# Folding q's weights in 32x32 tiles in the first token tile, and a new order around it

## The chip, the cores and the metric

The kernel runs on one core of a Trainium2 chip. The metric is the time of one execution on the device in microseconds (us). The kernel before took 374.88 us, the median of three runs (374.73 to 374.95). The engines are named as the profile does: PE (matrix products), PEld (PE's loads of the stationary operand), DVE, ACT and POOL (elementwise work), SP (which here only issues DMA transfers, in the order of its queue).

## What is computed

```python
# x: 2048 tokens x 512; 32 heads of 16 features
q, k, v = split_heads(x @ wqkv)
pq = einsum("bhsd,hdf->bhsf", q, w_phi)
pk = einsum("bhsd,hdf->bhsf", k, w_phi)
phi_q = concat([softmax(pq), softmax(-pq)])
phi_k = concat([softmax(pk), softmax(-pk)])
kv = einsum("bhsf,bhsd->bhfd", phi_k, v)
z = einsum("bhsf->bhf", phi_k)
num = einsum("bhqf,bhfd->bhqd", phi_q, kv)
den = einsum("bhqf,bhf->bhq", phi_q, z)[..., None] + 1e-6
a = merge_heads(num / den) @ wo
# second branch: per head the best of 16 keys on each side picks one of 256 experts
s1 = einsum("nhc,ec->nhe", x @ w_q[..., :128], k1)
s2 = einsum("nhc,ec->nhe", x @ w_q[..., 128:], k2)
e = argmax(s1) * 16 + argmax(s2)
b = sum over heads of gelu(x . u[e]) * v[e]
g = sigmoid((x * gate_w).sum(-1))
out = g * a + (1 - g) * b
```

## The kernel before

The 2048 tokens are cut into 16 tiles of 128. Every fp32 product is made of three products of a high and a low part (`mm3`), so each operand exists twice: `xh` and `xl`, `wah` and `wal`, `sh` and `sl`, `uh` and `ul`. One projection of a tile by 512 columns is 12 matmuls (4 blocks of 128 rows, 3 products each).

**Folded weights.** The key and query projections are not followed by `w_phi`; the product of the two weights is made once, on the chip, in `fold` (line 149), for k in the prologue and for q in tile 15. `fold` takes 64 matmuls of 32 rows, with the raw weights (`raw`) stationary and the small `wd` (32 columns made from `w_phi`, line 283) moving, into four banks (one for each group `q` of 8 heads), in two halves that are yielded one by one. ACT then casts them to `wah`, and DVE subtracts for `wal`. k's folded weights live in `wah` and `wal`; in tile 15 q's take their place.

**Score weights.** For the second branch the weights of `w_q` are multiplied with the keys in the same way (`score_w`, line 218): 16 loads of 1 MB (`wq0` to `wq15`, two buffers of the tag `st`, which the raw weights of k and q use as well), each multiplied in four matmuls with 512 columns, two loads to a bank `ws0` to `ws7`. A full bank goes through ACT as 16-bit planes (`score_planes`, line 226: `wpl`), is turned by a DMA transposition on SP (`wtp`), put together by ACT (`score_join`, line 233: `wtj`, then `sh`) and split by POOL (`sl`).

**The loop** (line 311) runs over the 16 tiles. Tile t loads x of tile t+3 (`x_load`), projects v (`vproj`, `pv`) and k (`kproj`, `pk`), takes the differences to the maximum and the minimum on DVE (`softmax_diffs`), the exponent on ACT, the sum, reciprocal and scaling (`ksoft`, line 196: DVE, DVE, POOL), and in every second tile adds two tiles to the sums of k and v (`kvacc`). The table `plan` (line 309) says how many loads of score weights each tile multiplies; after each, the load after next is issued on SP, where it waits until the product that reads its buffer is over. Everything is emitted under a schedule written by hand: each engine works its rows in the order of the program, and SP its transfers.

**The transition.** In tile 15 come the two halves of q's fold, between them the two halves of tile 0's scores (`front_s`: `s0`, `s1`), `kvacc(13)` and the sums of k for the last two tiles (`kvz`, line 211). Then the second loop runs tile by tile (`a` = 0 to 13, line 755) through q's projection (`front_q`), the projections to u and the gate (`front_p`, `pp`), the softmax of q, gelu, the choice of the experts, and the output product `po`. `z_split`, `z_rows` and `z_spread` (from line 695) bring the sum `z` into the rows that the denominators need.

## Time and profile before

| what | value |
|---|---|
| time, median of three runs | 374.88 us |
| time of the profiled execution | 375.19 us |
| its span, first to last instruction | 373.4 us |
| granted clock of PE | 1.000 |
| HBM read, written | 26.39 MB, 4.19 MB |
| mean traffic of the DMA engines | 125 GB/s |

The profile is of one execution. Its span begins with the first instruction and ends with the last; 1.8 us of the execution's time lie outside it. Busy times of engines overlap, so their sum says nothing; what counts is which engine's work and waits make up the chain that ended last. In the rows below and in the prediction, "x64" is a count of instructions in the trace; an fp32 matmul appears there twice, so that `fold`'s half of 32 matmuls is listed as 64. Names are the program's with the number left out (`foldq` is any of the four banks). "idle before, releaser" says how long the engine stood before these instructions, and which instruction of another engine released it.

### The profile page before, as it was taken

How to read it: one execution, taken by the hardware profiler on the slowest of the kernel's cores; microseconds unless marked ns; L12 is line 12 of the kernel's file. 1: busy time of each engine (PE TensorE's matmuls, PEld its weight loads, DVE VectorE, ACT ScalarE, POOL GpSimd, SP SyncE). 2: the span in 40 equal slices, each digit the busy share in tenths (PEclk: the TensorE clock that was granted, in tenths of full speed). 3: DMA queues.
4: the chain of work that ended last, by engine and by line, in shares of the span. 5: the costliest groups of instructions: out<-in, count | busy, mean ns of one | idle time of the engine just before them, and what ended most of it. 6: DMA issues, size and time to landing. Idle time of an engine off the chain costs nothing.

```text
span 373.4 us, 9179 instructions
## 1 busy us (share of the span) xinstructions
PE 367.6 (98%) x3680; PEld 294.3 (79%) x3680; DVE 314.4 (84%) x750; ACT 236.5 (63%) x421; POOL 161.5 (43%) x170
## 2 busy tenths in 40 slices
PE   8999999999999999999999999999999999999995
PEld 4767587787777888888888888888888888888874
DVE  4458878767767888999999999999999999999983
ACT  4243567437438544585876876966966966968752
POOL 2104363344343734573363453543643642743740
PEclk9999999999999999999999999999999999999999
DMA  7469894595695033143515434424326254245101
GB/s 269 172 235 300 226 305 173 147 303 180 169 289 194 4 87 80 35 101 77 103 20 84 110 60 84 101 58 98 89 69 100 70 87 98 62 96 100 58 29 58
DMA packets 71819, 46.52 MB, mean 125 GB/s; under 512 B 63200, under 2 KB 64096, under 8 KB 69472
## 3 DMA queue, kind: packets, MB, share of 16 engines
q1 hardware_dynamic: 70912, 45.17, 46.8%
q10 hardware_dynamic: 864, 0.76, 0.8%
q8 instruction: 29, 0.48, 0.5%
q14 instruction: 14, 0.11, 0.1%
HBM read 26.39 MB, written 4.19 MB: 82 GB/s over the span
## 4 chain that ended last, share of the span: by engine, by line
PE 93%; DMA 4%; ACT 1%; DVE 1%; issue 0%; ACTq 0%; DVEq 0%
PE po L629 17%; PE s L61 7%; PE s L60 7%; PE s L59 6%; PE pq L60 4%; PE pq L61 4%; PE pv L61 4%; PE ws L223 4%; PE pv L60 3%; PE pk L61 3%; PE pk L60 3%; PE pq L59 3%; PE pv L59 3%; PE oT L518 3%; PE s L57 3%; PE kvacc L207 2%
## 5 line engine op out<-in xcount | busy, mean ns | idle before, releaser
L439 POOL TENSOR_TENSOR w<-d,zb 128x512 f32<-128x512 f32 x32 | 40.8, 1296 | 80.6 <-ACT d L433 78.2
L200 POOL TENSOR_TENSOR d<-d,st 128x1024 f32<-128x1024 f32 x16 | 31.1, 1943 | 65.9 <-DVE st L199 58.5
L61 PE MATMUL s<-sh,xl 128*128 128x480 f32 x128 | 48.6, 380 | 0.0
L60 PE MATMUL s<-sl,xh 128*128 128x480 f32 x128 | 48.5, 379 | 0.0
L433 ACT ACTIVATE d<-d 128x512 f32<-128x512 f32 x32 | 20.0, 631 | 42.5 <-DVE d L109 34.1
L467 POOL TENSOR_TENSOR d<-d,st 128x512 f32<-128x512 f32 x30 | 31.3, 1064 | 23.0 <-DVE st L460 19.6
L509 ACT COPY pt<-tp 128x1024 uint16<-128x1024 uint16 x28 | 36.6, 1375 | 0.9 <-DMA tp<-pl 0.8
L59 PE MATMUL s<-sh,xh 128*128 128x480 f32 x96 | 36.4, 379 | 0.0
L353 ACT ACTIVATE d<-d 128x1024 f32<-128x1024 f32 x16 | 17.0, 1063 | 27.5 <-DVE d L111 27.5
L499 ACT COPY pl<-d 128x1024 uint16<-128x1024 uint16 x28 | 29.2, 1045 | 3.1 <-POOL d L467 3.1
L61 PEld LDWEIGHTS s<-sh,xl 128*128 128x128 f32 x128 | 24.0, 188 | 4.1
L60 PEld LDWEIGHTS s<-sl,xh 128*128 128x128 f32 x128 | 24.1, 188 | 3.3
L198 DVE TENSOR_REDUCE st<-d 128x64 f32<-128x1024 f32 x16 | 19.5, 1219 | 6.6 <-ACT d L353 6.3
L61 PE MATMUL pk<-wah,xl 128*128 128x480 f32 x64 | 24.3, 380 | 0.0
L60 PE MATMUL pk<-wal,xh 128*128 128x480 f32 x64 | 24.3, 379 | 0.0
L60 PE MATMUL pq<-wal,xh 128*128 128x480 f32 x64 | 24.3, 379 | 0.0
L61 PE MATMUL pq<-wah,xl 128*128 128x480 f32 x64 | 24.2, 379 | 0.0
L61 PE MATMUL pv<-wbh,xl 128*128 128x512 f32 x60 | 23.8, 397 | 0.3 <-DVE xl L145 0.3
L629 PE MATMUL po<-wbh,xh 128*128 128x512 f32 x60 | 23.7, 395 | 0.0
L629 PE MATMUL po<-wbl,xh 128*128 128x512 f32 x60 | 23.5, 392 | 0.0
L60 PE MATMUL pv<-wbl,xh 128*128 128x512 f32 x60 | 23.5, 392 | 0.0
L476 DVE TENSOR_TENSOR eq<-s,mx 128x512 bf16<-128x512 f32 x32 | 22.1, 692 | 1.1
(218 smaller groups left out, 1057.8 us busy)
## 6 DMA issues: line engine op xcount, KB each, us to landing
wq<-wq SPq DMA_DIRECT2D x16, 1024.0 KB, 6.8
xr<-xT SPq DMA_DIRECT2D x15, 256.0 KB, 6.2
y<-ot SPq DMA_DIRECT2D x15, 256.0 KB, 2.1
rawk<-wkT SPq DMA_DIRECT2D x1, 1024.0 KB, 6.4
rawq<-wqT SPq DMA_DIRECT2D x1, 1024.0 KB, 5.7
rawo<-wo SPq DMA_DIRECT2D x4, 256.0 KB, 3.9
rawu<-ug SPq DMA_DIRECT2D x2, 258.0 KB, 5.9
rawv<-wv ACTq DMA_DIRECT2D x2, 256.0 KB, 4.7
```

Of the source, the lines that this page charges most:

```text
L59: pe.matmul(o_, ah, bh[:, r], start=False, stop=False)
L60: pe.matmul(o_, ah, bl[:, r], start=False, stop=False)
L61: pe.matmul(o_, al, bh[:, r], start=False, stop=(last and i == n - 1))
L198: dve.tensor_reduce(st[:, 64:128], g64(d), axis=AX.X, op=ALU.add)
L200: pool.tensor_tensor(g64(d), g64(d), b64(st[:, 128:192]), op=ALU.mult)
L433: act.activation(hs(d, i), hs(d, i), AF.Exp)
L439: pool.tensor_tensor(hs(e["w"], i), hs(e["ph"], i), hs(zb, i), op=ALU.mult)
L467: eng.tensor_tensor(g64(d)[:, gs_], g64(d)[:, gs_], r[:, gs_].unsqueeze(2).to_broadcast([P, 32, F]), op=ALU.mult)
L476: dve.tensor_tensor(e["eq"][:, 512 * half:512 * half + 512].rearrange("p (h f) -> p h f", f=F), p3, mx.unsqueeze(2).to_broadcast([P, H, F] ...
L499: act.copy(pl, e["ph"][:, halves[i]].bitcast(U16).rearrange("p (c j) -> p j c", j=2))
L509: act.copy(p16[:, :, 4 * i:4 * i + 4, :], e["tp"][i].rearrange("p (j g) n -> p j g n", j=2))
L629: pe.matmul(h["po"], lhs(), rhs, start=first, stop=last)
```

## The change

q's fold moves from tile 15 to tile 0 and is computed another way. `fold_rows` makes the `wd` tile stationary and the raw weights moving: 16 matmuls of 32 rows by 32 columns of the array and 512 moving columns, one for each row group and output group, into four banks `foldq0` to `foldq3`. The result has features in rows, so it is turned like the score weights are: ACT writes planes, SP transposes them by DMA, ACT joins and casts to `wqh`, POOL subtracts for `wql`. Groups 0 and 1 are turned in tile 0, 2 in tile 2, 3 in tile 3; joined in tiles 2 to 5. q's folded weights have buffers of their own now; `uh`, `ul`, `eh` and `el` lie over k's weights (`shared`) and are split in tile 15, by ACT and POOL.

The raw weights of q take the first load's place, and the score weights follow one load later by a new table. `wpl` and `wtp` have two buffers each. x of tile 3 is split ahead of the loop by DVE; v of tile 3 moves to tile 2, of tiles 12 and 13 to tiles 13 and 14. `ksoft(14)` moves behind the differences of tile 15. In the transition `kvz(15)` stands between `pq0` and `pp0`, and `z_split`, `z_rows`, `z_spread`, `gelu_act(0)` and `back_cl(0)` change places.

```diff
+    shared = per.tile([P, 2 * NK * NU + 4 * D], F32R, name="shared")
+    wah, wal = part(0, NK, D), part(NK * D, NK, D)
+    uh, ul = part(0, NK, NU), part(NK * NU, NK, NU)
+    eh, el = part(2 * NK * NU, 2, D), part(2 * NK * NU + 2 * D, 2, D)
...
+    def fold_rows(raw):
+        for q in range(4):
+            qf[q] = tr_bank(f"foldq{q}") if q else mm_bank("foldq0")
+        for b in range(NK):
+            for q in range(4):
+                r = slice(32 * q, 32 * q + 32)
+                pe.matmul(qf[q][32 * b:32 * b + 32, :], wd[r, b, :], raw[r, b, :], start=True, stop=True,
+                          skip_group_check=True)
...
+    def turn_planes(src, n_):
+        pl = wa_.tile([P, 2, D], U16, tag="wpl", bufs=2, name=f"wpl{n_}")
+        act.copy(pl, src.bitcast(U16).rearrange("p (c j) -> p j c", j=2))
+        tp = wa_.tile([P, 8, P], U16, tag="wtp", bufs=2, name=f"wtp{n_}")
         sp.dma_start_transpose(tp, pl.rearrange("p j c -> p (j c)"))
+        return tp
+
+    def turn_join(tp, n_, hi, lo):
+        tj = wa_.tile([P, D], F32, tag="wtj", bufs=1, name=f"wtj{n_}")
         act.copy(tj.bitcast(U16).rearrange("p (k n j) -> p j k n", j=2, n=P),
                  tp.rearrange("p (j k) n -> p j k n", j=2))
+        t3 = tj.rearrange("p (k h e) -> p k h e", k=NK, e=F)
+        act.copy(hi, t3)
+        pool.tensor_tensor(lo, t3, hi, op=ALU.subtract)
...
-    raws = [stage(wq[0], "wq0")]
-    raws.append(stage(wq[1], "wq1"))
+    x_split(3)
+    raws = [stage(wqT, "rawq")]
+    raws.append(stage(wq[0], "wq0"))
...
-    plan = {0: 2, 2: 1, 3: 1, 4: 2, 6: 2, 8: 2, 10: 2, 12: 2, 13: 1, 14: 1}
+    plan = {2: 1, 4: 2, 5: 1, 6: 2, 7: 2, 8: 1, 9: 2, 10: 1, 11: 2, 12: 2}
...
+        if t == 2:
+            vproj(3)()
+        if t in (NT - 3, NT - 2):
+            vproj(t - 1)()
...
         for _ in range(plan.get(t, 0)):
-            score_w(done, raws[done])
+            score_w(done, raws.pop(0))
             done += 1
-            if done + 1 < 16:
-                raws.append(stage(wq[done + 1], f"wq{done + 1}"))
-            elif done == 15:
-                rawq = stage(wqT, "rawq")
+            used()
             if done % 2 == 0:
                 score_planes(done // 2 - 1)
+        if t == 0:
+            fold_rows(raws.pop(0))
+            used()
+            tq = []
...
-            for k in range(2):
-                split(eh[:, k, :], el[:, k, :], rawe[k], pool)
-            fq = fold(rawq, wah, wal, "q", False)
-            next(fq)
+        if t == NT - 1:
+            for k in range(NK):
+                split(uh[:, k, :], ul[:, k, :], rawu[k // 2][:, k % 2, :], pool)
+            split(eh[:, 0, :], el[:, 0, :], rawe[0], pool)
+            rawe.append(spare(ev[:, 1], "rawe1", [P, D]))
             front_s(0, 0)
-            next(fq)
             front_s(0, 1)
             kvacc(NT - 3)
-            next(fq)
+        if t == NT - 1:
+            ksoft(t - 1)
         act.activation(phis[t], phis[t], AF.Exp)
-        if t == 13:
-            for k in range(NK):
-                split(uh[:, k, :], ul[:, k, :], rawu[k // 2][:, k % 2, :])
-            rawe.append(spare(ev[:, 1], "rawe1", [P, D]))
-        ksoft(t)
+        if 1 < t < 6:
+            q_join(t - 2, tq[t - 2])
+        if t != NT - 2:
+            ksoft(t)
+        if t < 4:
+            tq += [q_planes(q) for q in ((0, 1), (), (2,), (3,))[t]]
```

Three places show how the order moves; two of them are on PE, one on SP. In a row, the number behind a name counts the program's tiles.

On PE before, around tile 12 (`ws6`, `ws7` the last two banks of score weights, of `wq12` to `wq15`; `pv13`, `pk13`, `pk14` projections, of which the first matmul of 12 is given):

```order
L223 MATMUL ws6_1219<-wq12_1051,kp_78 32x512 x4
L223 MATMUL ws6_1219<-wq13_1057,kp_78 32x512 x4
L207 MATMUL kvacc_98<-v9_977,d9_993 32x17 x32
L207 MATMUL kvacc_98<-v10_1024,d10_1040 32x17 x32
L57 MATMUL pv13_1308<-wbh_71,xh_61 128x512
L57 MATMUL pk13_1324<-wah_69,xh_61 128x512
L223 MATMUL ws7_1343<-wq14_1224,kp_78 32x512 x4
L57 MATMUL pk14_1368<-wah_69,xh_61 128x512
L223 MATMUL ws7_1343<-wq15_1230,kp_78 32x512 x4
```

And in the changed kernel, from the end of tile 11 to tile 13:

```order
L231 MATMUL ws6_1221<-wq12_1055,kp_75 32x512 x4
L231 MATMUL ws6_1221<-wq13_1104,kp_75 32x512 x4
L57 MATMUL pk12_1252<-shared_67,xh_61 128x512
L231 MATMUL ws7_1271<-wq14_1226,kp_75 32x512 x4
L231 MATMUL ws7_1271<-wq15_1232,kp_75 32x512 x4
L215 MATMUL kvacc_95<-v9_1018,d9_1034 32x17 x32
L215 MATMUL kvacc_95<-v10_1078,d10_1094 32x17 x32
L57 MATMUL pk13_1360<-shared_67,xh_61 128x512
L57 MATMUL pv12_1379<-wbh_68,xh_61 128x512
```

The products of `wq14` and `wq15` have moved up: one projection stands between them and the products of `wq12` and `wq13`, where two projections and two sums, and then another projection, stood before.

On SP, the transfers from the end of the prologue to tile 5 in the changed kernel (`xr` x tiles, `wtpq0` to `wtpq3` the transposed planes of q's fold, `wtp0` those of `ws0`):

```order
L135 DMA wq2_421<-wq 128x2048
L238 DMA_TRANSPOSE wtpq2_467<-wplq2_465 128x8x128
L141 DMA xr6_469<-xT 128x512
L238 DMA_TRANSPOSE wtpq3_502<-wplq3_500 128x8x128
L141 DMA xr7_504<-xT 128x512
L135 DMA wq3_545<-wq 128x2048
L238 DMA_TRANSPOSE wtp0_549<-wpl0_547 128x8x128
L135 DMA wq4_556<-wq 128x2048
L141 DMA xr8_632<-xT 128x512
L135 DMA wq5_673<-wq 128x2048
```

Before, the loads `wq2` to `wq4` had one transposition among them, that of `ws0`; now `wq3` stands behind that of `wtpq3`, which is issued once ACT has written the planes of group 3.

On PE at the transition, the changed kernel from tile 15's last sums to the first projection of u (first matmul of each projection; in the program before, 32 matmuls of `foldq` stood ahead of `s0_0` and 32 ahead of `s1_0`, and `kvz(15)` behind `pp0`):

```order
L57 MATMUL pk15_1507<-shared_67,xh_61 128x512
L57 MATMUL s0_0_1538<-sh_63,xh_61 128x512
L57 MATMUL s1_0_1551<-sh_63,xh_61 128x512
L215 MATMUL kvacc_95<-v13_1439,d13_1373 32x17 x32
L223 MATMUL kvacc_95<-ones_71,d14_1420 32x1 x32
L57 MATMUL pq0_1655<-wqh_65,xh_61 128x512
L223 MATMUL kvacc_95<-ones_71,d15_1520 32x1 x32
L57 MATMUL pp0_1700<-shared_67,xh_61 128x258
```

The sums of tile 14 by `ones` (fifth row) read `d14`, whose scaling now comes behind the differences of tile 15 on DVE.

## The prediction

> **What bounds the kernel now.** I read the page first, its busy times and the chain that ended last.

> ```profile
> PE 367.6 (98%) x3680; PEld 294.3 (79%) x3680; DVE 314.4 (84%) x750; ACT 236.5 (63%) x421; POOL 161.5 (43%) x170
> PE 93%; DMA 4%; ACT 1%; DVE 1%; issue 0%; ACTq 0%; DVEq 0%
> ```

> PE is busy for 98% of the span and carries 93% of the chain. Next come the waits of PE, which here is the whole answer, and the busy time of PE by stretches (columns: length, then busy and count for PE, PEld, DVE, ACT, POOL, clock, DMA share, GB/s).

> ```profile
> PE warm L269 <- POOL tab L253: 1.2, 1, 1.2
> PE pv L92 <- ACT wbh L49: 0.5, 1, 0.5
> PE pv L61 <- DVE xl L145: 0.3, 1, 0.3
> 20.40:43.00 22.60, 22.29 (x174) 15.51 (x173) 16.66 (x25) 9.92 (x12) 7.04 (x4) 1.00 0.91 289
> 43.00:336.70 293.70, 293.70 (x3038) 239.59 (x3042) 261.89 (x634) 196.57 (x341) 136.72 (x132) 1.00 0.47 114
> 336.70:373.40 36.70, 32.91 (x300) 26.69 (x299) 26.95 (x76) 22.44 (x52) 14.17 (x15) 1.00 0.23 62
> ```

> From 43 to 336.7 us PE never stands. In the loop's first four tiles it waits once, 0.3 us. So three rules follow. Matmul time taken out is worth its full length. Work taken off DVE and ACT in that stretch is worth nothing, since nothing there waits for them. And every new wait of PE is paid in full, since there is no slack behind it to swallow it.

> **What goes: the old fold at tile 15.** The chain has its two halves whole, and two windows hold them and a half of s of tile 0 alone.

> ```profile
> 118.03 1.92 PE foldq L163 x64
> 119.95 0.43 PE s L57
> 122.77 1.92 PE foldq L163 x64
> 124.69 0.43 PE s L57
> 118.03:127.51 9.48, 9.48 (x160) 8.10 (x162) 6.98 (x12) 7.33 (x10) 6.82 (x6) 1.00 0.12 24
> 144.16:146.78 2.62, 2.62 (x14) 2.25 (x12) 2.45 (x8) 2.59 (x5) 1.68 (x2) 1.00 0.44 100
> ```

> 9.48 - 2 x 2.62 = 4.24 us: two halves of the fold of 1.92 each, and 0.2 us each for the matmul behind, 0.43 long and not 0.22, because the array changes its tiling. Ten score-weight sites plus two halves make 12 such changes before; one new fold, ten sites and the sums of v and k of tiles 11 and 12, which now stand alone, make 12 after. So the 0.2s cancel and **-3.84** is left. The fold's four ACT casts and four DVE subtractions beside it were covered: PE waits for neither.

> **What comes: 16 matmuls of 32x32 tiles at tile 0.** No row has this form. The nearest: a score-weight product, four matmuls (8 in the trace) of the same 512 columns and type, running in four column tiles side by side; and oT, where eight tiles run at once.

> ```profile
> 100.67 1.85 PE ws L223 x16
> 102.52 1.14 PE kvacc L207 x79
> 103.66 0.43 PE pv L57
> 106.62 0.23 PE pk L57
> 109.24 1.00 PE ws L223 x8
> 163.73 0.67 PE L518 MATMUL oT<-pt,kvb 64*32 64x128 f32 x32
> ```

> A round of four costs 1.85 / 2 = 0.93. If all 16 tiles run at once, the 16 matmuls cost that plus some issue; if only four at a time, 4 x 0.93 = 3.7. oT speaks for more than four at a time: its 32 instructions of 128 columns are as many columns as a ws round's 8 of 512, but take 0.67 where the round takes 0.93. At oT's eight tiles and pace the new fold would cost 4 x 0.67 = 2.7, and at sixteen half of that, 1.34; by the ws row, whose instructions are as long as the new ones, 0.93. I take **+1.07**, near the ws row; bounds 0.93 and 3.7. Its evictions (planes, joins) lie on ACT, POOL and SP, beside full PE work; they cost nothing but where SP's queue hands them on, at tile 5 below. xl of tile 4 is made earlier, so the 0.3 us wait goes: **-0.3**.

> **Score weights closer together: tile 12.** Two 1 MB buffers serve these loads; a load starts when the product that reads its buffer is over. The DMA queue's rows and the loads issued in two windows around the pair that starts at S = 100.67:

> ```profile
> 101.73 1.19 SPq L134 DMA_DIRECT2D wq<-wq  x2
> wq<-wq SPq DMA_DIRECT2D x1, 1024.0 KB, 4.7
> wq<-wq SPq DMA_DIRECT2D x1, 1024.0 KB, 8.0
> DMA to landing us min/median/max: 4.7/6.8/8.6
> ```

> The first load is issued at S+1.06 and lands at S+5.76; the second is issued at S+1.92 (an issue takes 0.33) and, sharing the engines, lands at S+9.92. Before, their readers came at 109.24 (S+8.57) and at 113.07, with v, k and sums between. The changed order has only pk12 between the two pairs. PE has the pair done at S+1.85 and pk12 (106.62 to 109.24: 2.62, plus 0.2) at S+4.67. It waits 1.1 for wq14, works to S+6.7, and waits 3.2 for wq15: **+4.3**. Bounds: at the shortest landing in the trace, 4.7, for both, 1.1; at the longest, 8.6, for the second, 4.9. I take the rows of the pair, since this is the same event. Behind the waiting product stand the sums of tiles 9 and 10 and pk13; all of PE shifts.

> [...] The trace's pair took until S+9.92, 8.9 us after the first issue, and I stay with it.

> **A load behind a transposition: tile 5.** The load of wq3 may start when the first product of tile 4's pair has ended, but on SP it stands behind the transposition of q3's planes, the last of the new fold, and that waits for ACT. The starts of pk0 and of the product behind it, the pace of DVE, and what ACT and SP do for one such turn:

> ```profile
> 20.57 0.23 PE pk L57
> 23.20 1.90 PE ws L223 x16
> 28.86 0.63 DVE L105 TENSOR_REDUCE st<-pk 128x32 f32<-128x512 f32 x1
> 34.11 0.63 DVE L105 TENSOR_REDUCE st<-pk 128x32 f32<-128x512 f32 x1
> 35.84 0.68 DVE L111 TENSOR_TENSOR d<-st,pk 128x512 f32<-128x512 f32 x1
> L353 ACT ACTIVATE d<-d 128x1024 f32<-128x1024 f32 x16 | 17.0, 1063 | 27.5 <-DVE d L111 27.5
> L235 ACT COPY wtj<-wtp 128x1024 uint16<-128x1024 uint16 x8 | 10.8, 1351 | 2.7 <-DMA wtp<-wpl 2.5 <-POOL sl L241 0.2
> L240 ACT CAST sh<-wtj 128x512 fp32r<-128x512 f32 x8 | 9.0, 1125 | 0.3
> L228 ACT COPY wpl<-ws 128x1024 uint16<-128x1024 uint16 x8 | 8.1, 1012 | 8.9 <-PE ws L223 8.8
> 40.15 1.25 SPq L230 DMA_TRANSPOSE wtp<-wpl  x1
> ```

> DVE cycles a tile in 5.25 (28.86 to 34.11), so tile 3's differences start near 39.36 and end 2.41 later (34.11 to 36.52) at 41.8. ACT then does the exponent 1.06, the join of q1 1.35 + 1.13 and the planes of q3 1.01: 46.3. The transposition holds SP 1.25, the x tile's issue behind it some 0.4: wq3 goes out at 48.0. PE reaches its product at 23.20 + fold 1.27 + four pk (2.62) + pv3, pv4, pv5 (2.76: 106.62 less 103.66, less 0.2) + three score-weight products 2.85 + sums of tiles 0 to 2, 1.7 + two refills 0.4 + pk5 2.62 = 50.8. With landing times of 4.7 to 6.8, the wait is 1.9 to 4.0; nothing less unless ACT runs earlier. I take **+2.6**, a landing of 5.4, nearer the short end, since only the transposition and one x tile of 256 KB are in flight when it starts.

> Tiles 6 and 7 hold two pairs with the sums of tiles 3 and 4, pv7 and pk7 between: PE is at the last product at S + 1.85 + 1.34 + 2.76 + 2.62 + 1.0 = S+9.6, its load at S+9.92: **+0.4**, bounds 0 and 0.9.

> **Transition.** ksoft of tile 14 moves behind the differences of tile 15.

> ```profile
> L198 DVE TENSOR_REDUCE st<-d 128x64 f32<-128x1024 f32 x16 | 19.5, 1219 | 6.6 <-ACT d L353 6.3
> L199 DVE RECIPROCAL st<-st 128x64 f32<-128x64 f32 x16 | 8.9, 553 | 0.5
> L200 POOL TENSOR_TENSOR d<-d,st 128x1024 f32<-128x1024 f32 x16 | 31.1, 1943 | 65.9 <-DVE st L199 58.5 <-ACT wtj L235 7.4
> L401 POOL TENSOR_TENSOR x<-x,px 128x256 f32<-128x256 f32 x16 | 11.9, 746 | 3.7 <-ACT x L392 3.6
> L50 POOL TENSOR_TENSOR el<-rawe,eh 128x512 fp32r<-128x512 f32 x2 | 2.6, 1334 | 0.0
> ```

> With pk15 ended at T, d of tile 14 is scaled at T + 2.41 + 1.22 + 0.55 + 1.94 = T+6.1, T+6.3 with handovers. PE, two halves of s (5.24) and the sums of tile 13 (half of 1.14) later, needs it at T+5.8: **+0.5**. Behind it on PE stand pq0, the sums of tile 15 and pp0, in order. POOL has five pieces ahead of that scaling, u's split moved from DVE and half of the value table's: 4 x 0.75 + 1.33 = 4.3 by the rows of like size. u lies over k's weights now, so its casts wait until pk15 has read them, and the first pieces come free while pk15 runs; POOL is done near T+3.8, before the reciprocal at T+4.2. If none started before T, it would be T+4.7 and the wait 1.0; if handovers cost nothing, 0.3. The z steps, the gelu and the back part of tile 0 move on ACT, DVE and POOL only or to places where PE has 2.6 us of other matmuls ahead of them: nothing; if that cover failed anywhere, PE would stand there and the waits of PE would list it.

> **Sum.** -3.84 + 1.07 - 0.3 + 4.3 + 2.6 + 0.4 + 0.5 = +4.73 on a span of 373.4, so 378.1. The profiled execution took 375.19, 1.8 outside the span and 0.3 over the median of 374.88. I set the change on the median: **379.6 us**.

> **Rivals.** *wq3 in time.* ACT reaches q3's planes 3 us sooner, if exponents and joins overlap more than their mean times say. Against it stands the queue of DVE, which the 5.25 us cycle fixes. Without the terms of tiles 5 and 7: 379.6 - 3.0 = 376.6. Chance 0.16.

> *Faster: loads that keep their 4.7.* If the second load of a pair does not slow down, wq15 lands at S+1.92+4.7 = S+6.6, before PE needs it; the turning point is a landing of 4.8 us. Then tile 12 costs 1.1, tiles 5 and 7 at best nothing: -3.84 + 1.07 - 0.3 + 1.1 + 0.5 = -1.5, so 373.4. For it: the first of the pair took 4.7. Against it: the second took 8.0. Chance 0.10. With tile 5's wait at 1.9 beside it, 375.3, within the resolution: 0.05.

> *Four tiles at a time.* The fold costs 3.7: 382.2. The oT row speaks against it. Chance 0.08.

> *The clock falls in a gap*, or the transition waits longer. The clock reads 1.00 in each window, in the last one too, where PE idles 36.70 - 32.91 = 3.8 us in pieces. If a gap of 3.2 us at tile 12 halved it for as long again, about 3.4 us of matmuls would take 1.7 more: 381.3. Chance 0.06. [...]

> That the change doesn't do what it says holds in part within my forecast: it frees DVE and ACT at the transition, where no one waits for them.

> **How the numbers follow.** My forecast has 0.55. About 0.2%, 0.75 us, is what a measurement of this kernel can tell from no change. Faster: the second rival and a little of the first's spread, 0.11; within: its variant, 0.06; slower: the rest, 0.83. The range leaves out the fast rival below and the far ends above, 375.6 to 382.3; the likeliest case alone spans 378.2 to 381.2.

> **What will show it.** Right: waits of PE's weight loads for wq near 1.1 and 3.2 us at tile 12, 2 to 4 at tile 5; foldq as 32 instructions in about 1 us; kvz behind POOL by half a microsecond; clock 1.00. Wrong, if wq lands with PE not waiting at tile 12, if foldq takes over 2 us, or if PE idles past tile 15 for an engine that was free before.

## The result and the profile after

The changed kernel took 386.79 us, the median of four executions (385.03 to 392.81), against 374.86 before: a ratio of 1.030, 95% interval 1.024 to 1.037. The ratio leaves out the slowest execution, 392.81, as a slow one (the median of the other three is 385.16); the first profile fell in it, so the rows here are of the second one, 390.34 us with a span of 388.5. Run again beside other kernels it took 387.69 (385.35 to 390.34) against 374.96: 1.034 (1.028 to 1.040). The forecast was 379.6, with a range up to 382.3: the sign was right, the size outside.

The page, its busy times, the clock in 40 slices and the chain:

```profile
span 388.5 us, 8997 instructions
PE 371.7 (96%) x3584; PEld 294.8 (76%) x3584; DVE 310.6 (80%) x743; ACT 247.6 (64%) x428; POOL 170.4 (44%) x178
PEclk9999989999696999999999999999999999999999
PE 88%; DMA 7%; DVE 2%; ACT 1%; issue 1%; POOL 0%; ACTq 0%; DVEq 0%; POOLq 0%
```

PE's share of the chain fell from 93% to 88%, DMA's rose from 4% to 7%, and the clock, 9 in every slice before, shows 8, 6 and 6. PE has fewer instructions than before (3584 for 3680) and yet is busy 4.1 us longer. The whole list of PE's waits, and the rows of the products that wait (in brackets, the idle time before them):

```profile
PE ws L231 <- DMA wq<-wq: 7.8, 4, 3.3
PE pv L57 <- issue: 2.6, 1, 2.6
PE warm L290 <- POOL tab L274: 1.2, 1, 1.2
PE pv L93 <- ACT wbh L49: 1.1, 2, 0.6
PE kvacc L223 <- POOL d L208: 0.5, 1, 0.5
54.37 1.29 PE L231 MATMUL ws<-wq,kp 128*32 128x512 f32 x8 [3.27 <-DMA wq<-wq]
73.51 1.07 PE L231 MATMUL ws<-wq,kp 128*32 128x512 f32 x8 [1.36 <-DMA wq<-wq]
114.49 1.07 PE L231 MATMUL ws<-wq,kp 128*32 128x512 f32 x8 [1.27 <-DMA wq<-wq]
117.41 1.93 PE L231 MATMUL ws<-wq,kp 128*32 128x512 f32 x8 [1.85 <-DMA wq<-wq]
```

The four waits stand where the forecast had them: tile 5, tile 7 and twice tile 12, 7.8 us together where 7.3 were forecast. The wait of the sums of tile 14 for POOL is the 0.5 forecast. The stall of 2.6 us ahead of a v projection was not forecast at all; the last product took 1.93 and not 1.00.

The new fold, in the groups and in the chain; the load that PE waits for at tile 5, on SP and in the chain; and the last load, of tile 12, in the chain:

```profile
L178 PE MATMUL foldq<-rawq,wd 32*32 32x512 f32 x32 | 1.1, 600 | 0.0
23.47 1.07 PE foldq L178 x32
46.20 1.49 SPq L238 DMA_TRANSPOSE wtpq<-wplq  x1
47.78 0.53 SPq L141 DMA_DIRECT2D xr<-xT  x1
48.36 0.42 SPq L135 DMA_DIRECT2D wq<-wq  x1
48.36 5.96 DMA wq<-wq
110.46 6.90 DMA wq<-wq
```

The fold costs 1.07, as estimated. wq3 goes out at 48.36 (forecast 48.0), behind the transposition, and lands 5.96 later (forecast 5.4). The last load, the second of its pair, takes 6.90 (forecast 8.0).

So the sum without new effects is 373.4 - 3.84 + 1.07 - 0.3 + 7.8 + 0.5 = 378.6, half a microsecond over the forecast span of 378.1. The profile has 388.5. Of the 9.9 us that are left, 2.6 are the stall; 7.3 are something that makes PE's own work longer.

**The clock.** PE's busy time and clock in stretches of 3.4 us (columns as before: length, then busy for PE, PEld, DVE, ACT, POOL; then clock, DMA share, GB/s):

```profile
51.70:55.10 3.40, 0.73 (x8) 0.16 (x8) 1.98 (x4) 0.14 (x1) 3.30 (x3) 1.00 1.19 294
55.10:58.50 3.40, 3.40 (x11) 2.33 (x8) 0.97 (x2) 2.79 (x4) 0.00 (x0) 0.50 0.97 386
72.10:75.50 3.40, 2.04 (x16) 1.02 (x13) 1.64 (x3) 0.86 (x1) 1.15 (x2) 1.00 0.94 246
96.00:99.50 3.50, 1.43 (x132) 1.22 (x124) 3.07 (x6) 3.11 (x4) 0.00 (x0) 0.99 1.01 335
99.50:102.90 3.40, 2.82 (x7) 2.27 (x8) 1.28 (x2) 1.81 (x2) 1.91 (x2) 0.50 1.11 259
102.90:106.30 3.40, 3.40 (x10) 2.66 (x9) 0.00 (x0) 0.59 (x1) 1.65 (x3) 0.50 0.08 25
113.10:116.50 3.40, 1.18 (x9) 0.16 (x8) 3.37 (x6) 2.16 (x2) 1.53 (x1) 1.00 0.96 374
116.50:119.90 3.40, 2.49 (x68) 1.18 (x72) 0.63 (x2) 0.50 (x1) 1.92 (x2) 0.50 0.87 251
119.90:123.40 3.50, 3.50 (x90) 3.08 (x83) 2.14 (x3) 3.47 (x5) 0.00 (x0) 0.51 0.48 80
```

Three stretches in which PE is busy 0.73, 1.43 and 1.18 us of 3.4 are followed by half rate; the one with 2.04 is not. Half rate (a clock of 0.50) lasts one, two and two such stretches, five in all. In the clock records of the first profile the four falls are 3.413, 3.413, 6.827 and 6.826 us long. A v matmul of the chain takes 0.43 us in them and 0.23 elsewhere. PE is busy for 15.6 us of the five stretches; at full rate this work would take half, 7.8 us less, and 7.3 is what the sum lacks.

**The stall.** The projection is that of v for tile 11. Its row, the 5.2 us from 92.1, and the queue q8 in the list of DMA queues, where it stands as "instruction" (a tenth of a microsecond from 97.3, and the whole page):

```profile
100.08 0.77 PE L57 MATMUL pv<-wbh,xh 128*128 128x512 f32 x1 [2.65 <-issue]
92.10:97.30 5.20, 5.20 (x151) 3.87 (x149) 3.15 (x6) 1.52 (x3) 2.04 (x2) 1.00 1.04 370
q8 instruction: 1, 0.02, 65.1%
q8 instruction: 28, 0.46, 0.5%
```

In the first profile the same stall of 3.1 us is put down to ACT's copy into wtj. That name misleads: this matmul needs the high part of x of tile 11, which ACT had ready some 7 us earlier, and in the second profile nothing at all is named. The queue q8 has 28 packets of 16 KB here and had 29 before. PE's records in the trace, with the few instructions that the page leaves out, are 7,232 in the first profile and 7,423 before, 28.25 and 29.0 times 256. So by these counts there is one packet to 256 instructions of PE; that it brings them is an inference. The one that starts at 97.3 comes behind 5.2 us in which the DMA engines had a share of 1.04; it ends at 98.4, and PE goes on at 100.1. In the first profile the packet at this stall runs from 99.97 to 101.08, behind 3.0 us with a share of 1.01, and PE goes on at 102.5.

### The profile page after: what moved, and what is told of

It reads as the page before. It is cut to its first block, busy times and chain, and to the rows that moved or that the text cites. A ratio compares the mean times of both kernels' runs of the same rounds, so it can differ in the third digit from the quotient of the medians.

```text
span 391.0 us, 8997 instructions
## 1 busy us (share of the span) xinstructions
PE 373.5 (96%) x3584; PEld 295.0 (75%) x3584; DVE 310.6 (79%) x743; ACT 247.7 (63%) x428; POOL 170.6 (44%) x178
## 4 chain that ended last, share of the span: by engine, by line
PE 87%; DMA 8%; DVE 2%; ACT 1%; issue 1%; POOL 0%; ACTq 0%; DVEq 0%; POOLq 0%
PE po L661 15%; PE s L61 7%; PE s L60 7%; DMA wq<-wq 6%; PE s L59 5%; PE ws L231 4%; PE pv L61 4%; PE pv L60 4%; PE pq L60 4%; PE pq L61 3%; PE pk L60 3%; PE pk L61 3%; PE pv L59 3%; PE pq L59 3%; PE oT L550 2%; PE pk L59 2%
## 5 line engine op out<-in xcount | busy, mean ns | idle before, releaser
L61 PE MATMUL s<-sh,xl 128*128 128x480 f32 x128 | 48.6, 380 | 0.0
L106 DVE TENSOR_REDUCE st<-pk 128x32 f32<-128x512 f32 x16 | 10.7, 668 | 23.6 <-PE pk L61 23.6
L61 PEld LDWEIGHTS s<-sh,xl 128*128 128x128 f32 x128 | 24.0, 188 | 4.0
L231 PE MATMUL ws<-wq,kp 128*32 128x512 f32 x128 | 18.6, 679 | 8.6 <-DMA wq<-wq 8.6
L146 DVE TENSOR_TENSOR xl<-xr,xh 128x512 fp32r<-128x512 f32 (+2 forms) x17 | 11.9, 699 | 17.9 <-ACT xh L145 17.6
L61 PE MATMUL pv<-wbh,xl 128*128 128x512 f32 x60 | 25.0, 417 | 0.0
L60 PE MATMUL pv<-wbl,xh 128*128 128x512 f32 x60 | 25.0, 417 | 0.0
L60 PE MATMUL pk<-shared,xh 128*128 128x480 f32 x64 | 24.6, 384 | 0.0
L61 PE MATMUL pk<-shared,xl 128*128 128x480 f32 x64 | 24.4, 382 | 0.0
L60 PE MATMUL pq<-wql,xh 128*128 128x480 f32 x64 | 24.4, 381 | 0.0
L61 PE MATMUL pq<-wqh,xl 128*128 128x480 f32 x64 | 24.1, 377 | 0.0
## 6 DMA issues: line engine op xcount, KB each, us to landing
wq<-wq SPq DMA_DIRECT2D x16, 1024.0 KB, 6.0
rawk<-wkT SPq DMA_DIRECT2D x1, 1024.0 KB, 6.6
rawq<-wqT SPq DMA_DIRECT2D x1, 1024.0 KB, 7.1
```

What stands on the lines that cost most here:

```text
L60: pe.matmul(o_, ah, bl[:, r], start=False, stop=False)
L61: pe.matmul(o_, al, bh[:, r], start=False, stop=(last and i == n - 1))
L231: pe.matmul(wsP[j][32 * c:32 * c + 32, :], kp[:, j // 4, par, :], raw[:, c, :], start=(par == 0), stop=(par == 1))
```

## The experiments

The theories were: the waits for loads, each followed by a fall of the clock (theory 1), against a clock that is low for another reason (theory 2); and for the stall, PE out of instructions (theory F), against a late operand.

**The changed kernel again.** Unedited.

> The changed kernel once more, nothing edited, for a second profile and more times. Theory 1 (PE waits for wq four times, and after a gap PE is clocked down to half for stretches of 3.4 us, a number of stretches that differs from run to run): the same four waits, 8 to 9 us in all; the span is 379.8 us plus 1.7 for each stretch, so spans of 383.2, 384.9, 386.6 and so on, each with a mean clock lower by 0.0045 for a stretch. Theory 2 (the clock is low for a reason of the chip in that hour, not of the gaps): clock 1.00 in some runs with the same waits, the span then near 379.8. The wait of 3.1 us of pv11 that the first profile shows: if it belongs to the kernel, it stands here too.

The waits stand as above. Four executions had spans of 383.6, 384.5, 387.3 and 388.5 us at clocks of 0.991, 0.989, 0.982 and 0.978: each microsecond of span comes with a lower clock, though not in clean steps of 1.7. None had 1.00. The stall is there again, at the same matmul.

**Idle matmuls in the gaps.**

```diff
+    fills = {3: 12, 7: 7, 14: 5, 15: 9}
...
+            if done in fills:
+                if done != 15:
+                    idle = tr_bank(f"fill{done}")
+                for _ in range(fills[done]):
+                    pe.matmul(idle, xh[:, 0, 0, :], wbh[:, 0, :], start=True, stop=True)
             score_w(done, raws.pop(0))
```

> 33 idle matmuls of 512 columns, 0.23 us each, stand ahead of the four products that wait: 12 at tile 5 (2.7 us), 7 at tile 7 (1.6), 5 and 9 at tile 12 (1.1 and 2.0). The loads come no earlier. Theory 1: PE is busy through the gaps, the clock stays at 1.00, and the span falls to 379.5 to 381 us (time 381 to 383) with hardly a difference from run to run, though PE does more work. Theory 2: the clock falls as before, spans of 383 to 391; or, if the waits alone counted, no less than the fastest run of the changed kernel, 385.0.

The median was 384.84 (383.65 to 386.80). The clock did what theory 1 says: 1.000, 1.000, 0.998 and 0.996 in four executions, with nothing changed in the loads. Three of PE's waits in its profile (span 385.0):

```profile
PE pv L61 <- issue: 3.1, 1, 3.1
PE ws L231 <- DMA wq<-wq: 0.6, 2, 0.4
PE kvacc L223 <- POOL d L208: 0.5, 1, 0.5
```

The falls behind the waits at tiles 5 and 12 are gone, and so is that at tile 7, which the first profile has; the one stretch at half rate that is left follows the stall. The time missed its 381 to 383 because the stall stayed. It moved: it now stands inside v's projection of tile 7, ahead of the sixth of its twelve matmuls, the five before it having run on the same tile of x. No operand becomes late there. With 7.6 us of work added to PE (33 x 0.23), the kernel ran 2.9 us faster than without it.

**Group 3's planes a tile later.**

```diff
-        if t < 4:
-            tq += [q_planes(q) for q in ((0, 1), (), (2,), (3,))[t]]
+        if t < 5:
+            tq += [q_planes(q) for q in ((0, 1), (), (2,), (), (3,))[t]]
```

> The planes of q's group 3 are turned at the end of tile 4 and not of tile 3, so on SP the transposition stands behind the loads of wq3 and wq4. If the wait of tile 5 comes from that place in the queue, it goes (2.9 us in the profile), and with it one fall of the clock (1.7): 2.9 to 4.6 us less than the changed kernel in the median, so 382 to 384. If wq3 lands late for another reason (transfers that share the engines), the wait at tile 5 stays over 1.5 us and the time is that of the changed kernel.

380.05 (379.50 to 383.06), 1.015 times before (1.011 to 1.019): 7.6 us under the changed kernel, more than expected. The wait of 3.3 at tile 5 is gone, so the place of its load in SP's queue was the cause:

```profile
PE ws L231 <- DMA wq<-wq: 5.0, 3, 2.0
```

One of these three is new: 1.6 us at the last product of tile 6, whose load wq5 now stands behind the transposition. So a part of the wait has moved with the transposition. The stall for instructions is gone as well, which was no part of the edit: the packet in question came in time. That the loads around it had moved is the likely reason, and not shown. Between the two profiles, 10.0 us apart, waits for loads give 2.8, the stall 2.6, and two stretches at half rate in place of five the rest.

**No waits for loads.** Besides the line above, v of tile 12 goes back to its tile.

```diff
-        if 3 < t < NT - 4:
+        if 3 < t < NT - 3:
...
-        if t in (NT - 3, NT - 2):
+        if t == NT - 2:
...
-    plan = {2: 1, 4: 2, 5: 1, 6: 2, 7: 2, 8: 1, 9: 2, 10: 1, 11: 2, 12: 2}
+    plan = {2: 1, 3: 1, 4: 1, 5: 2, 6: 1, 7: 2, 8: 1, 9: 2, 10: 1, 11: 2, 12: 1, 13: 1}
```

> The planes of group 3 late as in q3late; v of tile 12 back in tile 12; and the score weights spread so that no two pairs stand in following tiles: one load each in tiles 2, 3, 4, 6, 8, 10, 12, 13, two in 5, 7, 9, 11. Theory 1: no wait for wq over 0.3 us, clock 1.00, and what is left is the smaller fold less two more refills and the wait at the transition: span 373.4 - 3.84 + 1.07 - 0.3 + 0.4 + 0.5 = 371.2, time 373.0, 0.5% faster than before. If the new fold, its turning or the new transition cost PE something that the profile does not show as a wait for wq, the time is 375 or more.

381.51 (379.67 to 382.92), not 373.0. Its waits show why:

```profile
PE kvacc L223 <- POOL d L208: 2.6, 1, 2.6
PE ws L231 <- DMA wq<-wq: 1.9, 2, 1.7
PE s L60 <- POOL sl L247: 0.7, 1, 0.7
```

The last product in tile 13 puts the last join into tile 14, and with it POOL's subtraction of 1.6 us right ahead of u's split and the scaling of d14. POOL at the transition has no room: the 0.5 us that the change costs there becomes 2.6. And wq4, behind other transfers, was 1.7 late. Beyond the 0.5 that was expected at POOL, these waits and one stretch at half rate (1.7) make up 6.4 of the 6.7 us between the profiled execution, 379.67, and the 373.0; the 1.8 us from there to the median are not profiled.

**The end of the table alone.**

```diff
-    plan = {2: 1, 4: 2, 5: 1, 6: 2, 7: 2, 8: 1, 9: 2, 10: 1, 11: 2, 12: 2}
+    plan = {2: 1, 4: 2, 5: 1, 6: 2, 7: 2, 8: 1, 9: 2, 10: 1, 11: 2, 12: 1, 13: 1}
```

(v of tile 12 goes back to its tile, as in the experiment above.)

> Only the end of the table and v of tile 12 are changed back: one load's product in tile 12 and the last in tile 13, v of tile 12 in tile 12. Two more projections' time stands between the products of wq12, wq13 and those of wq14, wq15. If the waits at tile 12 come from the spacing alone, they go (1.2 and 1.9 us in the second profile), with the fall of the clock behind them (6.8 us at half rate, 3.0 us lost): 6 us less than the changed kernel in the median, 381 to 382; the wait at tile 5 and its fall stay. If the waits are only moved to tile 13, the time stays over 385.

386.40 (385.42 to 388.50), 5 us over what was expected. The two waits of tile 12 went, but not the time:

```profile
PE ws L231 <- DMA wq<-wq: 3.7, 2, 2.7
PE pv L57 <- ACT wtj L243: 2.9, 1, 2.9
PE kvacc L223 <- POOL d L208: 2.6, 1, 2.6
```

The second row is the stall for instructions again, the first the waits of tiles 5 and 7. What tile 12 gave, the transition took: 2.6 us at POOL, 0.7 more for the last `sl`, and a stretch at half rate behind them. The changed kernel's tight pair at tile 12 bought room for POOL in tile 15.

**Other warming matmuls.**

```diff
-    for _ in range(16):
-        pe.matmul(wps[:, :384], warm[:, 1:P + 1], warm, start=True, stop=True)
+    for i in range(64):
+        c = slice(96 * (i % 4), 96 * (i % 4) + 96)
+        pe.matmul(wps[:, c], warm[:, 1:P + 1], warm[:, c], start=True, stop=True)
```

> The 16 warming matmuls of the prologue are cut into 64 of a quarter of the columns: 96 more instructions on PE ahead of everything else (48 loads of weights, 48 matmuls), the same columns. It is for the stall of 2.6 to 3.1 us at the first matmul of pv11, in which PE waits for no other engine. Theory F: PE ran out of instructions, since the transfer that brings the next 256 came late; then a stall, where there is one, begins after 256 x (i + 1.75) instructions of PE's trace (2241 and 1473 in the runs so far, i = 7 and 4), and pv11, now 96 instructions later, is not its place. Rival: something that pv11 needs comes late; then the stall stands at pv11's first matmul as before, at instruction 2337.

One execution: 381.99 us, 5.7 under the changed kernel's median, so that the size is rough. Neither expected place has a stall; there is none:

```profile
PE ws L231 <- DMA wq<-wq: 6.6, 5, 2.5
```

96 instructions in the prologue (which ends no later) take a stall of 3 us out of tile 11. That speaks against a late operand at pv11, whose work is unchanged. The eight stalls of over 0.5 us with no operand missing, in seven profiles of six kernels, begin after 1473, 2241 or 2753 instructions of PE: each 256 n + 193. In the first and second profile and in that of the idle matmuls PE went on 1.4, 1.7 and 1.4 us after a packet of q8 had ended. So theory F fits these counts; what makes a packet late is another question, and no experiment here settles it.

**Spread, with the old transition's order.**

```diff
+    plan = {2: 1, 3: 1, 4: 1, 5: 1, 6: 2, 7: 1, 8: 2, 9: 1, 10: 2, 11: 1, 12: 2, 13: 1}
...
-        if t == NT - 1:
-            ksoft(t - 1)
+        if t == NT - 2:
+            score_join(*old.pop())
         act.activation(phis[t], phis[t], AF.Exp)
...
-        if t != NT - 2:
-            ksoft(t)
+        ksoft(t)
```

(Group 3 late; v of tiles 4 to 13 in their tiles; both halves of the value table split after the loop.)

> A version meant to keep the fold's gain: planes of group 3 late; v of every tile from 4 to 13 in its own tile; products 1, 1, 1, 1, 2, 1, 2, 1, 2, 1, 2, 1 in tiles 2 to 13; the last join ahead of the exponent in tile 14; ksoft of tile 14 back in tile 14; the value table's low part after the loop. If waits for loads, the clock behind them, late instructions and POOL at the transition are all that the change costs, nothing of them is left: 373.4 - 3.84 + 1.07 - 0.3 + 0.4 (two more changes of tiling) = 370.7 of span, 372.5 in time, 0.6% under before, at clock 1.00. If instructions come late once, 3 us more and a fall of the clock 1.7: 375 to 377.

386.94 (384.60 to 388.74): my own order was no better. Its longest waits:

```profile
PE pv L57 <- ACT sh L246: 3.8, 1, 3.8
PE zT L730 <- DVE zc L726: 3.0, 1, 3.0
PE s L57 <- ACT sh L246: 1.2, 1, 1.2
```

The first is the stall at instruction 2241 (the name is again of no account); the others stand at the joins and at z's first step, where I had changed the order. Three stretches at half rate follow.

**Two more, with the changed kernel's transition.** Group 3 late, v of tile 12 in tile 12, the last product in tile 12; the second kernel with the warming matmuls cut as well.

```diff
-    plan = {2: 1, 4: 2, 5: 1, 6: 2, 7: 2, 8: 1, 9: 2, 10: 1, 11: 2, 12: 2}
+    plan = {2: 1, 3: 1, 4: 1, 5: 1, 6: 2, 7: 1, 8: 2, 9: 1, 10: 2, 11: 2, 12: 2}
```

> q3late, with v of tile 12 back in tile 12 and the products 1, 1, 1, 1, 2, 1, 2, 1, 2, 2, 2 in tiles 2 to 12; the last product stays in tile 12, and the transition is the changed kernel's. What is left of waits for loads should be some 0.2 us at tile 11 and 1.3 at tile 12, too short to bring a fall of the clock (no stretch of 3.4 us under half busy), and 0.5 at the transition: span 373.4 - 3.84 + 1.07 - 0.3 + 0.2 + 1.5 + 0.5 = 372.5, time 374.3. If instructions come late (a stall of some 3 us where PE has worked off 256 x (i + 1.75) instructions, and a fall of the clock behind it), 377 to 379. If the fold's gain is not there, over 377 without such a stall.

> mix, with the warming matmuls cut as in pad, so that the transfers of instructions come 96 instructions earlier in the program. Same sum: 374.3 without a stall for instructions. [...]

379.75 (377.13 to 382.47), 1.016 times before (1.009 to 1.023), and 378.30 (376.43 to 379.14), 1.009 (1.006 to 1.011): the best version, still slower than before. Neither reached 374.3. Two executions of the first, 377.1 and 377.6, took what was expected with a stall; the other two, 381.9 and 382.5 at clocks of 0.993 and 0.989, took more and are not profiled. The first one's profile is of its fastest execution, span 375.3, clock 1.000:

```profile
PE pv L57 <- ACT d L385: 1.6, 1, 1.6
PE ws L231 <- DMA wq<-wq: 1.4, 2, 0.9
PE kvacc L223 <- POOL d L208: 1.0, 1, 1.0
PE pk L61 <- issue: 0.6, 1, 0.6
```

Here the sum can be tested without the clock: 373.4 - 3.84 + 1.07 - 0.3 + 0.2 and the 4.6 of these rows make 375.1, and 375.3 was measured. So the fold's gain of 2.8 us is there in full; waits of 4.6 eat it. PE's busy time says the same: 365.2 us for 367.6 before, where -3.84 + 1.07 + 0.2 make 365.0. Two of the waits are stalls for instructions (2241 and 1473), which come and go with edits that have nothing to do with them; the second kernel had only a short one (0.7, at 2753). Both kernels have a stall, then, at different places: the shift of 96 instructions moves it, and doesn't by itself decide whether there is one.

No version tried beats the kernel before. A third buffer for the loads was not tried.

## Why the prediction was right and wrong

- **What bounds the kernel, and that every new wait is paid in full:** right. 2.8 us of fold went and 8.3 of waits came, and nothing later gave any of it back.
- **-3.84, +1.07, -0.3:** right. The fold measured 1.07, to the hundredth by luck, since it was taken between bounds of 0.93 and 3.7; the 0.2s of the changes of tiling did cancel to within 0.2, by the sum of the last experiment.
- **Tile 12, +4.3:** the two waits are there, 1.27 and 1.85: 3.1. The first is the forecast 1.1; the second is shorter than 3.2 because the second load took 6.90 and not 8.0. In both profiles of the changed kernel this pair goes out 0.86 us apart; the second load took 6.90 and 7.24, and both were over 7.8 and 8.1 after the first issue. So the one pair of before, 8.9, was a poor measure. Why the pair of before took longer is open.
- **Tile 5, +2.6:** 3.3, by a landing 0.6 later. That the transposition ahead of it is the cause is shown: moved, it takes the wait along.
- **Tile 7, +0.4:** 1.36. The pair's second load took 9.0 where the row of before has 8.0. A transposition and an x tile were in flight with it; that they are the cause is not shown.
- **Transition, +0.5:** 0.5. The experiments show how near to a far larger wait this is.
- **The four waits together:** 7.8 where 7.3 were forecast. That is nearer than the terms, which were off by -1.2, +0.7 and +1.0: in part luck.
- **The clock:** here the forecast failed. The sum has no term for it. The rival "the clock falls in a gap" had 0.06 and a price of one stretch at half rate, 1.7, for one gap, an estimate with no row of before behind it; it happened, beside the forecast case and not in its place, after two of the waits for loads and the stall, for 7.3 us. What spoke against it was the tail of before: a clock of 1.00 though PE idles 3.8 us "in pieces". That row was misread. Up to 369.6 PE has no idle piece; the 3.8 us are one, behind its last matmul, and half rate follows once the span is over:

```profile
336.70:369.60 32.90, 32.90 (x300) 26.69 (x299) 26.66 (x75) 21.98 (x51) 14.17 (x15) 1.00 0.22 57
370.50:373.90 3.40, 0.00 (x0) 0.00 (x0) 0.00 (x0) 0.00 (x0) 0.00 (x0) 1.00 0.33 116
373.90:375.40 1.50, 0.00 (x0) 0.00 (x0) 0.00 (x0) 0.00 (x0) 0.00 (x0) 0.51 0.00 0
```

  So the trace of before showed no gap of over 0.5 us in mid-work that the clock had survived, and no price of one. In the two profiles of the changed kernel single gaps of 2.3 to 3.3 us were enough, and at tile 12 pairs of 1.2 and 2.2 or 1.3 and 1.9, where one stretch was over half idle; the gap of 1.36 at tile 7 was not, nor was one of 2.5 at tile 5 with the cut warming matmuls (a clock of 1.00 there). Half rate followed stretches of 3.41 us in which PE was busy up to 1.39, and of 3.4 up to 1.43. By the second profile each of the three gaps that brought it has a price of one or two stretches, 1.7 to 3.4 us, on top of its length.
- **The late instructions:** the forecast has no term for them, and put no wait of PE at this place: 2.6 us, and 3.1 of the 7.3 at half rate, half of the 2.82 and 3.40 us that PE worked in the two stretches behind the stall. q3late and the cut warming matmuls, in which the stall is absent, are 7.6 and 5.7 us faster.
- **Rivals:** loads that keep 4.7 us, four tiles at a time, wq3 in time: all out, each by its own row above. The chances were put on cases that exclude each other; the ones that came true add up.

## What to carry to other kernels

Price a new gap on an engine that is otherwise full at its length plus what the clock did after such gaps: line up PE's busy time in stretches and compare. Here, of 3.4 us, stretches with 0.67 to 1.43 us of PE's work were followed by half rate and one with 2.04 was not, and a stretch at half rate cost up to 1.7. When an order is made tighter, look at what the looser order left free: time for two loads in flight, and POOL ahead of the transition. And read a releaser against the program: if an engine stops in the middle of work whose operands are all there, count its instructions too: the stalls here began after 1473, 2241 and 2753 of them.
